# An attention pair's fine scores beside the next pair's coarse ones, and new costs for the planner of a two-stage kernel

## The chip, the cores and the metric

The kernel runs on one core of a Trainium2 chip. Its engines work side by side, each through its own queue in order: TensorE (PE in the profile; PEld is its weight load), VectorE (DVE), ScalarE (ACT), GpSimd (POOL), and SyncE (SP), which here issues all DMAs. The metric is device time in microseconds of one execution.

## The reference, cut to what matters

```python
B, H, S, D = 8, 8, 576, 64                   # q, k, v are (B, H, S, D) float32
q_d, k_d, v_d = (x.reshape(B, H, 144, 4, D).mean(axis=3) for x in (q, k, v))
out_d  = sm_attn(q_d, k_d, v_d)              # softmax(q k^T / 8) v over 144 pooled positions
out_up = np.repeat(out_d, 4, axis=2)
mask   = np.abs(pos[:, None] - pos[None, :]) < 4
scores = np.where(mask, q @ k^T / 8, -1e9)   # a band of 7 positions
out_local = softmax(scores) @ v
x = (out_up + out_local).transpose(0, 2, 1, 3).reshape(4608, 512)
h = x @ w_in                                 # w_in (512, 2048)
y = (h - tanh(h)) @ w_out                    # w_out (2048, 512); y is the output
```

## The kernel before, in words

**Two stages.** The attention makes the 4608 x 512 matrix x, kept transposed as four tiles `xT` (one for each pair of heads, channels on partitions, all tokens beside each other). The dense stage multiplies it by w_in and w_out in 9 blocks of 512 tokens.

**Attention.** 64 heads are worked off as 32 pairs, four pairs to a batch, two pairs to a group (16 groups). For a group, q and k are loaded in four DMAs to `qkn` (`load_qk`), cast to bf16 with an exchange of axes (`reorder`, L441: q and k apart, i = 0 and 1), transposed on TensorE (`turn`, L457, nine matmuls), copied out of PSUM to `qk` (L463), and pooled by two adds, `half` (L473) and `qkd` (L478). For pair p, `attention(p)` then runs: `s1`, the band scores of four of the five query tiles (8 matmuls, L508); exp of them (L547, 128x960) and multiplication by the 0/1 mask (L551); `s2`, the band scores of the fifth tile and the pooled scores (6 matmuls, L508 and L527); exps of these (L562, 128x192, and L565, 128x576) and a small mask (L569); `outs`, 18 matmuls of the probabilities by v and pooled v (L580, L586); reciprocal (L595) and scaling to `ln` (L597). Up to pair 11 `ln` is transposed on TensorE (`back`, L631 to L635), copied by ScalarE (`od`, L638) and added to `xT` by VectorE (L640). From pair 12 (`XOUT`) on a DMA transposes it and VectorE adds the two parts (L616).

**PSUM.** Two tiles of two banks each, `ps_ts` and `ps_ox`, serve the attention ("ts" and "ox" in the code; the first batch has a second pair of them), four banks `ps_hy` the dense stage. Up to pair 13, `s1` and `s2` of a pair are two operations that both write `ps_ts`. From pair 14 (`MERGE`) on they are one operation, `both`, which writes `s1` to `ps_ts` and `s2` to `ps_ox`.

**Dense.** `mm1` (L663) makes a 128 x 512 piece of h from four matmuls; ScalarE takes tanh (L672), VectorE subtracts to `gT` (L675). `mm2` (L691) accumulates 16 matmuls to a 128 x 512 piece of y; ScalarE copies it (L702) and SyncE stores it (L705).

**Weights** come as float32 in eight quarters (`load_w`), are kept in tiles that are free at that time (`gT`, and a part of `xT`), and are cast in pieces of 128 x 512 (L397). The queue of loads is: groups 0 and 1 and their v, w_in, groups 2 and 3, w_out, groups 4 and on. From group 9 on, a load waits until pair 2n - 5 has issued its output transpose (the key `fl`, with `AHEAD` = 5).

**What sets the order.** Nothing is issued as it is written. Each step is registered with `op(engine, ns, function, reads, writes, pri)`, or with `choice` where several engines could do it (casts, copies, adders). `Program.order` then plays the whole program through: it takes for each engine the ready step of the lowest `pri`, lets it last its `ns`, and lets users on other engines start after the engine's `LAT` (L25). The order of these planned starts is the order in which the instructions are put into the engines' queues; on the chip semaphores make them wait for their inputs, and nothing passes another in a queue. Dense matmuls have `pri` 5000, so they fill what attention leaves on TensorE. `spare` (L32, L243) adds to the lag for steps of high `pri`: 2500 ns after a DMA and 1000 ns after POOL, from `pri` 140 on. `pri` is 10 for each pair or 20 for each group. In `load`, the DMA's cost is the planned transfer time (`T_QK`, `T_V`, `T_W`; transfers are planned one behind the other). In gaps of TensorE before the first dense matmul, `filler` (L867) puts matmuls on a tile `warm`, whose result nobody reads.

**The loop** over pairs (L836 on) registers, for each p, the values' cast, scores, the transposes of group n + 1 where `INNER` and `OUTER` say so (from pair 8 on the one with i = p % 2), outputs, and at odd p the next group's loads; after each batch it registers the dense blocks that have become possible.

Of the kernel before, what the change touches and what calls it, by code (L numbers as in the profile page):

```python
# [9 lines left out]
BF16 = mybir.dt.bfloat16  # L10
# [5 lines left out]
class Program:  # L16
# [10 lines left out]
    def __init__(self):  # L27
        self.ops = []
        self.alternatives = {}
        self.touch = []  # L30
        self.fresh = set()
        self.spare = (5000, {})  # L32
        self.last_write = {}
        self.readers = {}
# [27 lines left out]
    def order(self):  # L62
# [16 lines left out]
        for _ in range(n):  # L79
            best = None  # L80
            for eng, cand in ready.items():
                if not cand:
                    continue
                now = max(free.get(eng, 0.0), min(at[i] for i in cand))
                if eng == "DMA":
                    pick = min((at[i], i) for i in cand)[1]
                else:
                    pick = min((self.ops[i][4], i) for i in cand if at[i] <= now)[1]
                if best is None or now < best[0]:
                    best = (now, eng, pick)  # L90
            now, eng, i = best
            if i in self.alternatives:
                for other in self.alternatives[i]:
                    ready[other].remove(i)
                self.ops[i] = self.alternatives[i][eng] + self.ops[i][3:]
            else:
                ready[eng].remove(i)
            start[i] = now
            end = now + self.ops[i][1]
            free[eng] = end  # L100
            for u in users[i]:
                same = self.ops[u][0] == eng and eng != "DMA"
                lag = self.LAT[eng]
                if self.spare[0] <= self.ops[u][4] < 5000:
                    lag += self.spare[1].get(eng, 0)
                at[u] = max(at[u], end if same else end + lag)
                left[u] -= 1
                if left[u] == 0:
                    make_ready(u)
# [45 lines left out]
def kernel(  # L155
# [9 lines left out]
    nc = tc.nc  # L165
# [76 lines left out]
    P = Program()  # L242
    P.spare = (140, {"DMA": 2500, "POOL": 1000})  # L243
    op = P.op
# [50 lines left out]
    def load(ns, fn, keys, cost, pri, after=()):  # L295
        op("SP", ns, fn, reads=after, writes=list(keys) + ["queue", ("q", keys[0])],
           pri=pri)
        op("DMA", cost, None, reads=[("q", keys[0])], writes=keys, pri=pri)

    def slot_qk(n):  # L300
        return n % 2 if n >= GV else n % NQKN

    def load_v4(n):

        b, h0 = n // 2, 4 * (n % 2)
        base = v[b, h0]
        for i, (g0, m) in enumerate(((0, 128), (128, 16))):
            rows = bass.AP(tensor=base.tensor, offset=base.offset + 4 * D * g0,
                           ap=[[4 * D, m], [S * D, 4], [1, 4 * D]])
            to = v4[128 - m:128, i]  # L310
            load(650, lambda to=to, rows=rows: nc.sync.dma_start(out=to, in_=rows),
                 [("qkn", 2, i, y) for y in range(2)], (1100, 350)[i], -30,
                 [("fl", 2 * n - AHEAD)])
# [18 lines left out]
    def load_qk(n):  # L332

        b, h0, s = n // 2, 4 * (n % 2), slot_qk(n)
        for i, src in enumerate((q, k)):
            for y in range(2):
# [7 lines left out]
                def issue(to=to, rows=rows):  # L344
                    nc.sync.dma_start(out=to, in_=rows)  # L345
                load(650, issue, [("qkn", s, i, y)], T_QK, -30,
                     [("fl", 2 * n - AHEAD)])

    def load_v(p):

        b, j, s = p // NP, p % NP, p % NVST
        t = vst[s]
# [24 lines left out]
    def load_w(src, dst, name, f, stage, keys):  # L377

        def issue():
# [4 lines left out]
            else:  # L384
# [4 lines left out]
                else:  # L389
                    nc.sync.dma_start(  # L390
                        out=stage.rearrange("p (c f) -> p c f", c=4),
                        in_=rows[:, 4 * f:4 * f + 4, :])
        load(600, issue, keys, T_W, -30)
        for c in range(4):
# [7 lines left out]
    def prep_v(p):  # L402
        s, w, jj = p % NVST, (p // 2) % NVW, p % 2
        P.choice([(eng, ns, lambda fn=fn: fn(  # L404
# [5 lines left out]
    def pool_v(hb):  # L410
# [6 lines left out]
        def mm():  # L417
# [7 lines left out]
           writes=[key], pri=pri)  # L425
        op("ACT", 300, lambda: A.copy(
            out=vd[w][:, :, :, 0:64],
# [18 lines left out]
    def turn(n, i):  # L446
# [5 lines left out]
        pri, cold = 20 * n, (1.5 if n < 1 else 1.0)  # L452
        b16 = ps.rearrange("p n c -> p (n c)").bitcast(BF16)[:, 0:A6 * 128]

        def tr():
            for a in range(A6):
                T.transpose(b16[:, 128 * a:128 * a + 128], qr[s][:, i, a, :], ident)  # L457
        P.fresh.add(len(P.ops))
        op("PE", 480 * cold, tr, reads=[("qr", s, i), "ident"], writes=ts, pri=pri)
        o = qk[s][:, :, KOFF * i:KOFF * i + 576]  # L460
# [15 lines left out]
        def add2(eng):  # L476
            with nc.allow_low_precision("pooled q and k"):
# [4 lines left out]
        P.choice([(name, n2, lambda eng=eng: add2(eng)) for name, _, n2, eng in adders],  # L482
                 reads=["half"], writes=[("qkd", s, i)], pri=pri)

    def attention(p):
# [43 lines left out]
        qks = [("qk", sq, i) for i in range(2)]  # L529
        pad = ["bias", "ident"] if first else []  # L530
        yield
        P.fresh.add(len(P.ops))
        if first:
            op("PE", 480, lambda: off(0, 480, 0), reads=pad, writes=ts, pri=pri)
        qkds = [("qkd", sq, i) for i in range(2)]
        if p >= MERGE:
            def both():
                s1()
                s2()
            op("PE", 800, both, reads=qks + qkds, writes=ts + ox, pri=pri)  # L540
        else:
            op("PE", 420 * cold, s1, reads=qks, writes=ts, pri=pri)
# [7 lines left out]
        if not first:  # L550
            op("DVE", 700, lambda: V.tensor_tensor(  # L551
                out=e1, in0=e1,
# [4 lines left out]
        if first:  # L557
            op("PE", 100, lambda: off(480, 96, 0), reads=pad, writes=ts, pri=pri)
        if p < MERGE:
            op("PE", 380 * cold, s2, reads=qks + qkds, writes=ts, pri=pri)  # L560
        sb = ox if p >= MERGE else ts
# [6 lines left out]
        if not first:  # L568
            op("DVE", 220, lambda: V.tensor_tensor(  # L569
                out=e2v, in0=e2v,  # L570
# [111 lines left out]
    def mm2(kb, i):  # L682
# [16 lines left out]
        if part == 3:  # L699
# [7 lines left out]
               reads=[("y", ys)], writes=[("yq", ys)], pri=-1)  # L707
            op("DMA", 1000, None, reads=[("yq", ys), ("y", ys)], pri=-1)

    def dense(kb):  # L710
# [13 lines left out]
        for i in range(16):  # L724
            if kb < NBLK:
# [4 lines left out]
    M2_FIRST = 16  # L730
    XOUT, T_OUT, AHEAD = 12, 2000, 5
    MERGE, GV = 14, 7
    XADD = [("DVE", (800, 350), V)]
    ORDER, W_FIRST = "g0123", "0123g"
    INNER, OUTER = {4: [0], 5: [1]}, {3: [0, 1], 7: [0, 1]}
    T_QK, T_V, T_W, W_PRI, NEARLY = 760, 800, 2750, 33, NP
    CAST = [("POOL", 700, GP.tensor_copy), ("ACT", 520, A.copy)]
    CAST_V = [[("POOL", 720, GP.tensor_copy), ("ACT", 640, A.copy)],
              [("POOL", 790, GP.tensor_copy)]]
    any3 = [("DVE", 860, V.tensor_copy), ("ACT", 950, A.copy),  # L740
            ("POOL", 1350, GP.tensor_copy)]
    REORDER = [[any3, any3], [any3[0:1], any3[2:3]]]
    TURN = [[("ACT", 1125, A.copy), ("DVE", 1250, V.tensor_copy)],
            [("ACT", 1125, A.copy)]]
    ADDERS = [[("DVE", 750, 440, V), ("POOL", 1190, 750, GP)],
              [("POOL", 1190, 880, GP)]]
# [89 lines left out]
    for p in range(NPAIR):  # L836
# [5 lines left out]
        if p >= 2:  # L842
            next(work[p])
        inner = INNER.get(p, [p % 2] if p >= 2 * NP else [])
        outer = OUTER.get(p, [])
        for i in inner if n + 1 < NGRP else []:
            reorder(n + 1, i)
            turn(n + 1, i)
        next(work[p], None)
        for i in outer:  # L850
            reorder(n + 1, i)
            turn(n + 1, i)
        if p % 2 == 1:
# [47 lines left out]
```

## Time and profile before

| | |
|---|---|
| median of 13 runs | 344.22 us (343.2 to 348.7) |
| the profiled execution: time, span | 345.8 us, 344.1 us |
| mean granted clock of TensorE in it | 0.978 |
| `mm1` and `mm2` matmuls, busy (records overlap) | 144.6 and 141.6 us |
| tanh L672, subtraction L675 | 0.600 us and 0.685 us each, 144 of each |
| DMA, 0 to 94 us; after that | share near 1.0; 0.06 to 1.04 |
| POOL's last work | about 250 us |

The page divides the span into 40 slices of 8.6 us. A digit is the busy share of a slice in tenths; in the row PEclk it is the granted clock of TensorE. A row of windows gives the stretch, its length, the busy time with the number of instructions of each engine asked for, the granted clock, the DMA share and GB/s. A row of waits reads: who waited for whom, total us, how often, the longest. In a timeline the columns are start, duration (of several instructions: from the first start to the last end), engine, line, operation, output and input, count, and in brackets how long the engine had been idle and what ended it. Matmuls of TensorE overlap; a matmul's record is longer than the distance to the next.

### The profile page before, as it was taken

What the parts mean: (1) busy time and instruction counts of PE and PEld (TensorE: products, weight loads), DVE (VectorE), ACT (ScalarE), POOL (GpSimd) and SP (SyncE); (2) the same over time, 40 slices, a digit from 0 to 9 for tenths busy, and PEclk for the clock granted to TensorE, in tenths of its full rate; (3) what the DMA queues carried; (4) which work ended last, traced back from release to release, by engine and by line L of the source; (5) the groups of instructions that cost most, each with busy time, mean ns of one, the idle gap of its engine ahead of it and who ended that gap; (6) DMA issues with size and microseconds to landing.
All of it is one profiled execution on the core that took longest, in us unless ns stands there. A gap on an engine that the chain in (4) does not pass through costs nothing.

```text
span 344.1 us, 6786 instructions
## 1 busy us (share of the span) xinstructions
PE 323.4 (94%) x2570; PEld 169.4 (49%) x2616; DVE 214.4 (62%) x360; ACT 204.7 (60%) x342; POOL 152.3 (44%) x179
## 2 busy tenths in 40 slices
PE   4886999998999999999999999999999999999995
PEld 1562554554565554545455555454544444444442
DVE  4766674658997678678676668766676453344300
ACT  2675897558868575756667656665765244344411
POOL 8434865595885066748483838492300000000000
PEclk9696999999999999999999999999999999999999
DMA  7998999999902397969898869862222200100021
GB/s 218 257 388 261 246 337 326 259 291 284 289 17 58 105 253 217 224 164 213 225 180 227 188 178 221 222 175 59 59 57 60 57 30 32 60 32 32 30 85 68
DMA packets 84749, 57.51 MB, mean 167 GB/s; under 512 B 62638, under 2 KB 67822, under 8 KB 84718
## 3 DMA queue, kind: packets, MB, share of 16 engines
q1 hardware_dynamic: 84718, 57.09, 60.8%
q8 instruction: 20, 0.33, 0.4%
q14 instruction: 11, 0.09, 0.1%
HBM read 43.05 MB, written 9.44 MB: 153 GB/s over the span
## 4 chain that ended last, share of the span: by engine, by line
PE 79%; DMA 10%; DVE 3%; SPq 3%; ACT 2%; issue 2%; ACTq 0%; DVEq 0%
PE ps_hy L663 33%; PE ps_hy L691 33%; DMA qkn<-in_q_dram 6%; PE ps_ts L457 3%; DMA gT<-in_moe_w_in_dram 3%; PE ps_ts L508 2%; PE ps_ox L580 2%; PE ps_ox L586 2%; SPq L369 2%; DMA qkn<-in_k_dram 1%; DVE ln L597 1%; SPq L345 1%; ACT uy L672 1%; PE ps_ox L527 1%; DVE qr L441 1%
## 5 line engine op out<-in xcount | busy, mean ns | idle before, releaser
L663 PE MATMUL ps_hy<-xT,w_in_sb 128*128 128x512 bf16 x555 | 144.6, 383 | 5.6 <-DVE xT L640 3.7
L691 PE MATMUL ps_hy<-w_out_sb,gT 128*128 128x512 bf16 x552 | 141.6, 379 | 2.1 <-issue 1.1
L675 DVE TENSOR_TENSOR gT<-ps_hy,uy 128x512 bf16<-128x512 f32 x144 | 95.8, 685 | 57.0 <-ACT uy L672 56.3
L672 ACT ACTIVATE uy<-ps_hy 128x512 f32<-128x512 f32 x144 | 83.8, 600 | 78.5 <-PE ps_hy L663 76.5
L663 PEld LDWEIGHTS <-w_in_sb 128*128 128x128 bf16 x576 | 53.9, 99 | 64.0 <-issue 7.3
L691 PEld LDWEIGHTS <-gT 128*128 128x128 bf16 x576 | 53.4, 98 | 59.7 <-issue 0.3
L473 POOL TENSOR_TENSOR half<-qk 128x576 f32<-128x576 bf16 x29 | 34.6, 1193 | 57.3 <-ACT qk L463 56.6
L463 ACT COPY qk<-ps_ts 128x1152 bf16<-128x1152 bf16 x28 | 31.5, 1126 | 15.6 <-PE ps_ts L457 13.5
L702 ACT COPY uy<-ps_hy 128x512 f32<-128x512 f32 x36 | 21.2, 588 | 21.7 <-PE ps_hy L691 20.7
L597 DVE TENSOR_TENSOR ln<-ps_ox,r 128x896 bf16<-128x896 f32 x30 | 32.7, 1090 | 0.9
L547 ACT ACTIVATE E<-ps_ts 128x960 bf16<-128x960 f32 x30 | 29.2, 974 | 6.8 <-PE ps_ts L508 6.7
L551 DVE TENSOR_TENSOR E<-E,mask 128x960 bf16<-128x960 bf16 x28 | 22.1, 789 | 11.1 <-ACT E L547 10.7
L404 POOL CAST vw<-vst 128x640 bf16<-128x640 f32 x31 | 24.0, 785 | 9.5 <-DMA vst<-in_v_dram 7.8
L457 PEld LDWEIGHTS <-qr 128*128 128x128 bf16 x288 | 20.1, 104 | 12.7 <-DVE qr L441 5.6
L322 POOL TENSOR_TENSOR qkn<-qkn 128x512 f32<-128x512 f32 (+1 forms) x18 | 24.1, 1337 | 4.3 <-DMA qkn<-in_v_dram 3.2
L441 DVE CAST qr<-qkn 128x1152 bf16<-128x1152 f32 x18 | 15.8, 877 | 13.1 <-DMA qkn<-in_q_dram 9.8
L478 POOL TENSOR_TENSOR qkd<-half 128x288 bf16<-128x288 f32 x30 | 22.5, 750 | 2.4 <-DVE half L473 1.3
L457 PE MATMUL ps_ts<-ident,qr 128*128 128x128 bf16 x252 | 19.1, 222 | 4.1 <-DVE qr L441 2.6
L441 POOL CAST qr<-qkn 128x1152 bf16<-128x1152 f32 x14 | 17.0, 1218 | 8.1 <-DMA qkn<-in_k_dram 7.7
L616 DVE TENSOR_TENSOR xT<-lnT 128x480 bf16<-128x480 bf16 (+1 forms) x40 | 20.6, 528 | 0.0
L595 DVE RECIPROCAL r<-ps_ox 128x14 f32<-128x14 f32 x30 | 7.3, 243 | 20.8 <-PE ps_ox L586 18.9
L580 PE MATMUL ps_ox<-vw,E 128*128 128x65 bf16 x300 | 18.4, 194 | 1.0 <-DVE E L569 1.0
(86 smaller groups left out, 252.5 us busy)
## 6 DMA issues: line engine op xcount, KB each, us to landing
vst<-in_v_dram SPq DMA_DIRECT2D x62, 160.0 KB, 5.2
qkn<-in_q_dram SPq DMA_DIRECT2D x32, 288.0 KB, 3.5
qkn<-in_k_dram SPq DMA_DIRECT2D x32, 288.0 KB, 4.9
out_dram<-uy SPq DMA_DIRECT2D x36, 256.0 KB, 2.0
qkn<-in_v_dram SPq DMA_DIRECT2D x9, 512.0 KB, 5.3
gT<-in_moe_w_in_dram SPq DMA_DIRECT2D x4, 1024.0 KB, 11.8
xT<-in_moe_w_out_dram SPq DMA_DIRECT2D x8, 256.0 KB, 5.3
gT<-in_moe_w_out_dram SPq DMA_DIRECT2D x2, 1024.0 KB, 10.7
```

The costliest lines, as they stand in the source:

```text
L322: op("POOL", 1330, lambda t=t: GP.tensor_tensor(out=t[:, :, 0:2], in0=t[:, :, 0:2], in1=t[:, :, 2:4], op=ALU.add), writes=keys, pri=pri)
L441: P.choice([(eng, ns, lambda fn=fn: fn(out=dst, in_=srt)) for eng, ns, fn in REORDER[n >= 2][i]], reads=[("qkn", sn, i, x) for x in range(2)],
L457: T.transpose(b16[:, 128 * a:128 * a + 128], qr[s][:, i, a, :], ident)
L463: fn(out=o.rearrange("p y (g a) -> p y g a", a=A6), in_=b16.rearrange("p (a g y) -> p y g a", a=A6, y=2))
L473: eng.tensor_tensor(out=half, in0=four[:, :, :, 0:2], in1=four[:, :, :, 2:4], op=ALU.add)
L547: op("ACT", 980, lambda: A.activation(out=e1, in_=ps[:, :, 0:480], func=AF.Exp, scale=SCALE), reads=ts, writes=[("E", se, 0)], pri=pri)
L580: T.matmul(po[:, hh, 65 * t:65 * t + 65], E[se][:, c:c + 128], vw[w][:, 2 * jj + hh, t, :], start=True, stop=True)
L597: op("DVE", 1090, lambda: V.tensor_tensor(out=ln[sl].rearrange("p n (h d) -> p h n d", d=D), in0=blocks[:, :, :, 0:64], in1=r[s].unsqueeze ...
L663: T.matmul(ps_hy[slot], w_in_sb[:, dc, fc * 128:(fc + 1) * 128], xT[dc][:, kb * 512:kb * 512 + 512], start=(dc == 0), stop=(dc == N_DC - 1))
L672: op("ACT", 490, lambda: A.activation(out=u[us], in_=ps_hy[slot], func=AF.Tanh), reads=[("hy", slot)], writes=[("u", us)], pri=-1)
L675: op("DVE", 620, lambda: V.tensor_tensor(out=gT[g][:, fc, :], in0=ps_hy[slot], in1=u[us], op=ALU.subtract), reads=[("hy", slot), ("u", us) ...
L691: T.matmul(ps_hy[slot], gT[g][:, fc, ts * 128:ts * 128 + 128], w_out_sb[:, fc, :], start=(fc == 0), stop=(fc == N_FF - 1))
```

## The change

1. `MERGE` goes from 14 to 12, and the merged block is another one. From pair 12 on, `both` holds `s1` of pair p + 1 (to `ps_ts`) and `s2` of pair p (to `ps_ox`). Pair 12's own `s1` stands alone, and so does the last pair's `s2`.
2. From pair 12 on, the transposes of a group are registered earlier (`EARLY` = 12): both of group 7 at pair 12, and from there i = 0 of group n + 2 at odd pairs, and i = 1 of group n + 1 at even pairs, where before group n + 1 had one at each.
3. `spare` becomes a function of priority, engine and user. After a DMA: 1500 ns from `pri` 80 on, 2500 from 140. For users on TensorE, from `pri` 120 and from 180: POOL 1000 and 1500, VectorE 300 and 800, ScalarE 200 and 500. For other users: POOL 500 and 1000.
4. Planned costs change: q and k loads 760 to 900 (the k loads of group 0 by 400 more), v 800 to 780, the first two quarters of w_in by 300 and 1400 more, pooled v's loads, output stores 1000 to 750, output transposes 2000 to 1600, the masks 700 to 900 and 220 to 450, several casts and copies.
5. VectorE becomes a choice for the weights' casts.
6. A way to transpose q and k by DMA is added for groups from `FI` on, with a function `slot_v`; `FI` is 99, and there are 16 groups.

In the queues that result, the weights' 32 casts stand 15 on POOL, 9 on ScalarE, 8 on VectorE (before 18, 14, 0); the 32 casts of q and k 17 on POOL and 15 on VectorE (before 14 and 18); 18 filler matmuls (before 10). Every other matmul is there as before. The order of the loads on SyncE is the same; stores stand differently among them.

```diff
-    P.spare = (140, {"DMA": 2500, "POOL": 1000})
+    def spare(pri, eng, to):
+        if eng == "DMA":
+            return 2500 if pri >= 140 else 1500 if pri >= 80 else 0
+        level = (pri >= 120) + (pri >= LATER)
+        return SPARE[to == "PE"].get(eng, (0, 0, 0))[level]
+    LATER = 180
+    SPARE = ({"POOL": (0, 500, 1000)},
+             {"POOL": (0, 1000, 1500), "DVE": (0, 300, 800), "ACT": (0, 200, 500)})
...
+    def slot_v(p):
+        return p % 4 if p >= 2 * FI else p % NVST
...
-                load(650, issue, [("qkn", s, i, y)], T_QK, -30,
+                load(650, issue, [("qkn", s, i, y)],
+                     T_QK + (400 if n == 0 and i == 1 else 0), -30,
...
-        load(600, issue, keys, T_W, -30)
+        load(600, issue, keys, T_W + (W_LATE[f] if src is moe_w_in else 0), -30)
...
-        op("ACT", 300, lambda: A.copy(
+        op("ACT", 600, lambda: A.copy(
...
+        if n >= FI:
+            op("SP", 900, lambda: nc.sync.dma_start_transpose(
...
+        if n < FI:
+            P.fresh.add(len(P.ops))
+            op("PE", 480 * cold, tr, reads=[("qr", s, i), "ident"], writes=ts, pri=pri)
...
+        nexts[p] = s1, qks
...
-        if p >= MERGE:
-            def both():
-                s1()
-                s2()
-            op("PE", 800, both, reads=qks + qkds, writes=ts + ox, pri=pri)
-        else:
+        if p <= MERGE:
             op("PE", 420 * cold, s1, reads=qks, writes=ts, pri=pri)
...
-            op("DVE", 700, lambda: V.tensor_tensor(
+            op("DVE", 900, lambda: V.tensor_tensor(
...
-        if p < MERGE:
-            op("PE", 380 * cold, s2, reads=qks + qkds, writes=ts, pri=pri)
+        if MERGE <= p < NPAIR - 1:
+            ahead, more = nexts[p + 1]
+
+            def both():
+                ahead()
+                s2()
+            op("PE", 800, both, reads=qks + qkds + more, writes=ts + ox, pri=pri)
+        else:
+            op("PE", 380 * cold, s2, reads=qks + qkds, writes=ox if p >= MERGE else ts,
+               pri=pri)
...
-    XOUT, T_OUT, AHEAD = 12, 2000, 5
-    MERGE, GV = 14, 7
+    XOUT, T_OUT, AHEAD = 12, 1600, 5
+    MERGE, GV = 12, 7
+    FI, T_IN, EARLY = 99, 2050, 12
...
-    T_QK, T_V, T_W, W_PRI, NEARLY = 760, 800, 2750, 33, NP
-    CAST = [("POOL", 700, GP.tensor_copy), ("ACT", 520, A.copy)]
+    W_LATE = [300, 1400, 0, 0]
+    T_QK, T_V, T_W, W_PRI, NEARLY = 900, 780, 2750, 33, NP
+    CAST = [("POOL", 620, GP.tensor_copy), ("ACT", 620, A.copy),
+            ("DVE", 400, V.tensor_copy)]
...
-        inner = INNER.get(p, [p % 2] if p >= 2 * NP else [])
-        outer = OUTER.get(p, [])
+        inner = INNER.get(p, [] if p < 2 * NP else [p % 2] if p < EARLY else
+                          [0, 1] if p == EARLY else [1] if p % 2 == 0 else [])
+        m = n + 1 + (p > EARLY)
+        outer = OUTER.get(p, [0] if p > EARLY and p % 2 else [])
```

## The prediction

> **What bounds the kernel now.** I read the page's table of slices first, then stages by windows, then TensorE's waits and the timelines around them. The profiled execution took 345.8 us (its span is 344.1); the median of the 13 runs is 344.22, so that execution is 1.6 us above it. My sum is made against 345.8 and its difference carried to 344.22.
>
> ```profile
> span 344.1 us, 6786 instructions
> PE 323.4 (94%) x2570; PEld 169.4 (49%) x2616; DVE 214.4 (62%) x360; ACT 204.7 (60%) x342; POOL 152.3 (44%) x179
> PE   4886999998999999999999999999999999999995
> PEclk9696999999999999999999999999999999999999
> ```
> ```profile
> 36.00:82.00 46.00, 42.78 (x397) 1.00 1.01 290
> 82.00:262.00 180.00, 177.72 (x1560) 1.00 0.66 167
> 262.00:344.00 82.00, 77.19 (x367) 0.99 0.14 49
> ```
>
> TensorE has work nearly always. A dense matmul starts every 0.216 us ("0.86 us for x4" in the chain), so the 1152 of them alone need 249 us, and the order of TensorE's queue is fixed by the planner. The time is therefore TensorE's work plus the places where its next instruction is not ready. From 82 to 262 us (a row of the second fence: busy 177.7 of 180) I find only missing records, no waits. The losses are in three places: the start up to 36 us; three waits between 57 and 80 us; one at 275 us.
>
> The middle:
>
> ```profile
> PE ps_ox L580 <- DVE E L569: 1.0, 1, 1.0
> PE ps_ox L631 <- DVE ln L597: 0.9, 1, 0.9
> PE ps_ts L508 <- ACT qk L463: 0.7, 1, 0.7
> ```
> ```profile
> 58.10 1.02 DVE L441 CAST qr<-qkn 128x1152 bf16<-128x1152 f32 x1 [2.91 <-DMA qkn<-in_q_dram]
> ...
> 59.31 1.09 DVE L597 TENSOR_TENSOR ln<-ps_ox,r 128x896 bf16<-128x896 f32 x1
> ...
> 60.46 0.23 PE L631 MATMUL ps_ox<-ident,ln 128*128 128x128 bf16 x1 [0.95 <-DVE ln L597]
> ```
>
> VectorE stood 2.91 us in front of a cast whose load had not landed; pair 5's `ln`, whose input was ready before 57 us, was queued behind it, and TensorE waited 0.95 us. The other two have the same root or a like one: a cast waiting 2.87 us for q from 75.45 to 78.32 us holds up the mask of pair 8 (1.0 us lost), and a full-width `half` on POOL, queued behind a memset of 0.95 us, holds up ScalarE's `qk` copy (0.7 us lost). Together **2.6 us**.
>
> **The early start.** Weights, not TensorE, set it:
>
> ```profile
> 25.05 0.62 ACT L397 CAST w_in_sb<-gT 128x512 bf16<-128x512 f32 x1 [2.10 <-DMA gT<-in_moe_w_in_dram]
> ...
> 25.57 0.27 ACT L638 COPY od<-ps_ox 128x144 bf16<-128x144 bf16 x1
> ...
> 25.88 0.76 DVE L640 TENSOR_TENSOR xT<-ps_ox,od 128x576 bf16<-128x576 bf16 x1 [0.97 <-ACT od L638]
> ...
> 27.39 0.81 PE L663 MATMUL ps_hy<-xT,w_in_sb 128*128 128x512 bf16 x2 [2.54 <-DVE xT L640]
> ```
>
> ScalarE stands at a cast of the second quarter of w_in until it lands at 25.03; the `od` copy of pair 1 waits behind it, then `xT`, then the first dense matmul. The same happens again with the third quarter (landed 27.74): `od` of pair 3 at 29.63, eight dense matmuls from 30.75.
>
> **The change, part by part.**
>
> *Planned load times.* With its costs laid end to end, the planner of before expects the third and fourth quarter of w_out at 46.9 and 49.7 us and group 4's q and k from 50.5 to 52.7. The trace lands them at 53.9, 56.6 and 57.3 to 59.7: six or seven us late. With the new costs the plan has 51.1, 53.9 and 54.8 to 57.5, and from group 4 on (priority 80 and more) 1.5 us of slack on top. In the changed order of VectorE the cast of group 4's q stands behind `ln` of pair 5 and both masks of pair 6 (before: in front of pair 5's `ln`), that of group 6 behind `ln` of pair 7 (before: in front of it), that of group 7 behind the `ln` of pair 8 and the large mask of pair 9 (before: in front of pair 8's second mask). On POOL the memset now stands behind group 4's first `half`. All three waits lose their cause: -2.6. What is late next: TensorE comes 2.6 us earlier to group 5 and later; group 5's first transpose stands at dense matmul 124, about 70 us, its q landed by 63.4; group 6's at 168, about 83 us, landed by 73. Hidden.
>
> *w_in and the start.* The changed queues still hold a w_in cast in front of `od`: on ScalarE one of the second quarter, then `od` of pairs 2 and 1, then two of the third, then `od` of pair 3; VectorE has one of the second quarter ahead of `r` of pair 3. By the rows above: landing 25.03, cast to 25.65, `od` 2 and 1 to 26.25, `xT` of 2 and 1 to about 27.5 (2 x 0.76), `ln` of pair 3 to 28.6, its transposes to 29.0, `od` behind the casts of the third quarter (27.76 + 2 x 0.57 = 28.9), `xT` to between 30.1 and 30.7. The first dense matmul at 27.5 instead of 27.39, the steady run from 30.2 to 30.7 instead of 30.75: **0**, ends +0.3 and -0.6. That q and k casts move from VectorE (0.76) to POOL (1.14) and ScalarE's copies (1.12) to VectorE (1.36) at the start lies in front of the same landing; cover of at least 2 us.
>
> *Eight more filler matmuls* (18 for 10), all before the first dense one. Row: the granted clock is 0.50 from 8.2 to 15.0 us, after a stretch (4.8 to 8.2) with 1.11 of 3.40 us busy; again 0.50 from 28.7 to 35.5, after 0.79 of 3.40. [...] I take 0 for both.
>
> *Merged blocks from pair 12 on, fine scores of p beside coarse scores of p+1.* The same matmuls; two pairs more without a separate entry, about 0.1 us each: -0.2. The wait that matters is from the block to the pair's outputs (`O`). Before, 10 to 16 dense matmuls stand between, most often 12 and a transpose, as the big exp (0.97) and mask (0.79) must fit. Now 6 to 12, at the tightest 8, or 6 and a transpose: 0.22 + 8 x 0.216 = 1.95 us from the fine scores' start. The chain to fit is now only the small exps and the small mask. Nearest row: pair 4, fine scores at 44.23, exps ended 45.44, `O` at 46.19 after the same distance: 0.76 us spare. One dense evacuation in front (tanh 0.60, subtraction 0.685) still fits. Cost 0; ends 0 and +7 (third rival).
>
> *Earlier transposes after pair 12* (up to 72 dense matmuls earlier). Loads of group n still wait for the output transpose of pair 2n-5. Row: that pair's `O` at 161.25, transpose issued 163.48, q landed 168.9, k 171.8; with a cast (0.88 and 1.22) 8.5 and 11.8 us. The changed distance is at least 52 dense matmuls to the q transpose (11.2 us) and 64 to the k one (13.8), not counting the attention between. Hidden with 2 us to spare; if that is gone, TensorE waits the excess once per group, seven times.
>
> *End of attention.* The last `O` stands at dense matmul 786 instead of 810, the block that needs it still at 836: cover grows from 26 to 50 matmuls, 10.8 us. In the trace the short cover makes the planner bunch 14 L663 matmuls at 275 us, and
>
> ```profile
> 275.59 3.46 PE L663 MATMUL ps_hy<-xT,w_in_sb 128*128 128x512 bf16 x14 [0.67 <-ACT uy L702]
> ```
>
> The changed order has the regular alternation there: **-0.8** (0.67, and the stumble before and after it).
>
> *A new tight place.* At dense matmul 214 pair 11's back-transposes are followed by only a transpose, two matmuls and the pooling (1.6 us) before a matmul that needs its `xT` (`od` 0.28, `xT` 0.76, two hand-overs, 1.2 or more with VectorE's queue). Between 0 and +0.8; I take +0.2.
>
> *Dead parts.* FI = 99 is above the 16 groups: the DMA transpose of q and k is never emitted, and `slot_v` is p % 6 as before.
>
> Sum: -2.6 + 0 + 0 - 0.2 - 0.8 + 0.2 = **-3.4**: 342.4 for the profiled execution, 340.8 for the median.
>
> **The rivals.** (1) *Main case*, 340.8, own range 339.3 to 342.5: chance 0.55. [...] 0.15. (3) *The loads decide anyway*: DMA is at a share of 1.01 from 36 to 82 us, so TensorE, once early, waits for groups 5 to 7; only the 1 us of the end and merges remains, 343.2. Against it: the spare of 6 us and more at groups 5 and 6. 0.12. (4) *Slower: merged blocks too close to the outputs.* Place: the 20 `O` blocks of pairs 12 to 31. If a `qk` copy (1.12 us) stands ahead of the small exps in ScalarE's queue, the 0.76 us are overdrawn by about 0.36; at a mean 0.35, 20 x 0.35 = 7.0, and 340.8 + 7.0 = 347.8. It decides above a mean of 0.17 us per block (3.4 / 20). For it: such copies are one per pair, and ScalarE is busy 107 of 165 us there. Against it: slack planned for TensorE's inputs, 0.2 to 0.5 us from ScalarE and 0.3 to 0.8 from VectorE. 0.18.
>
> **How the numbers follow.** 0.3% is 1.0 us, about what a measurement of this kernel can tell from no change. Faster: nearly all of (1), (2), half of (3): 0.74. Same: 0.07. Slower: (4) with a little of the rest: 0.19. The range 337.3 to 345.5 takes in (2) and (3), the ends of the start and of pair 11, and the milder half of (4).
>
> **What would show it.** TensorE's three waits between 57 and 80 us gone, and no VectorE cast that waits over 1 us with `ln` or a mask behind it; no dense matmul that waits for a copy of L702 near 270; the first run of eight and more dense matmuls still near 30.5 us and a half-clock stretch there; the waits of `O` for exps and masks from pair 12 on below 1 us in all. The forecast is wrong if those waits sum to over 3 us, if waits for q, k or v appear between 60 and 90 us, or if the dense run begins before 29 or after 32 us.

## The result, and the profile after

The changed kernel takes **341.58 us** (median of 11 runs, 339.82 to 343.49); the kernel before, timed beside it, takes 344.9 (48 runs). The ratio is **0.9895, 95% interval 0.9873 to 0.9918**. The forecast, 340.8 against 344.22, was a ratio of 0.990. The profiled execution took 341.42 us (span 339.7, granted clock 0.995), where that of before took 345.8 (344.1, 0.978). One run of a later kernel (`merge_undone`, 428.15 us at a mean clock of 0.754) was in a slow state and is left out of its median.

The page's head, its row of engines and two rows of its table of slices, after:

```profile
span 339.7 us, 6802 instructions
PE 323.4 (95%) x2578; PEld 168.3 (50%) x2624; DVE 229.6 (68%) x369; ACT 199.6 (59%) x334; POOL 157.2 (46%) x178
PE   7786999999999999999999999999999999999995
PEclk9997999999999999999999999999999999999999
```

TensorE's busy time is the same to a tenth of a microsecond; the span has lost 4.4 us of idle or half-clock time. In the PEclk row the two dips of before (6 in the second slice, 6 in the fourth) have become one 7 in the fourth. The row says nothing of the first 9.26 us, where the trace's record of the clock has not begun: nine transposes that take 1.14 us at 5.87 us and 0.67 at 9.51 show TensorE at half speed there. Mean clocks leave out such a head too (0.995 is what the one stretch of 3.4 us at half clock, 29.74 to 33.15, makes of the record behind 9.26 us). The windows, with TensorE alone:

```profile
36.00:82.00 46.00, 45.11 (x426) 1.00 0.98 280
82.00:262.00 180.00, 177.52 (x1555) 1.00 0.68 171
262.00:344.00 82.00, 73.64 (x336) 0.99 0.12 43
```

From 36 to 82 us TensorE's idle time is 0.9 us instead of 3.2. From 82 to 262 the 2.5 us without a record are mostly missing records: another execution of the same program, taken later, has 32 records more there and this window table:

```profile
36.00:82.00 46.00, 45.83 (x432) 1.00 1.00 283
82.00:262.00 180.00, 179.66 (x1587) 1.00 0.69 169
```

TensorE works 225.5 of 226 us. What is left is the start, and 3.7 us at the end (77.5 us from 262 to the span's end, 73.8 busy), while the last results are copied and stored. TensorE's waits say the same. First 36 to 82 us (before: 1.0, 0.9 and 0.7 us for E, `ln` and `qk`), then 82 to 262 us, in the first changed profile:

```profile
PE ps_hy L692 <- issue: 0.3, 2, 0.2
PE ps_hy L720 <- issue: 0.2, 1, 0.2
```
```profile
PE ps_ox L432 <- DVE xT L669: 0.3, 1, 0.3
PE ps_ox L609 <- DVE E L598: 0.2, 1, 0.2
PE ps_hy L720 <- issue: 0.2, 1, 0.2
PE ps_hy L692 <- issue: 0.2, 1, 0.2
```

All three waits of the middle are gone. `O` (L609 now) waited once for a mask, 0.2 us. At the end of the attention the two dense products alternate and nothing waits for an evacuation (timeline of TensorE, after; before, 14 matmuls stood together at 275.59 behind a wait of 0.67):

```profile
272.82 1.89 PE L720 MATMUL ps_hy<-w_out_sb,gT 128*128 128x512 bf16 x8
274.55 1.89 PE L692 MATMUL ps_hy<-xT,w_in_sb 128*128 128x512 bf16 x8
276.27 1.03 PE L720 MATMUL ps_hy<-w_out_sb,gT 128*128 128x512 bf16 x4
```

The start, pair 3's way to the dense run (timeline of all engines, after):

```profile
27.14 1.08 DVE L626 TENSOR_TENSOR ln<-ps_ts,r 128x896 bf16<-128x896 f32 x1
28.28 0.23 PE L660 MATMUL ps_ts<-ident,ln 128*128 128x128 bf16 x1 [0.63 <-DVE ln L626]
...
28.90 0.28 ACT L667 COPY od<-ps_ts 128x144 bf16<-128x144 bf16 x1 [1.11 <-PE ps_ts L664]
29.22 0.76 DVE L669 TENSOR_TENSOR xT<-ps_ts,od 128x576 bf16<-128x576 bf16 x1 [0.99 <-ACT od L667]
...
30.03 4.93 PE L692 MATMUL ps_hy<-xT,w_in_sb 128*128 128x512 bf16 x15 [1.21 <-POOL w_in_sb L410]
```

From the two `xT` before this `ln` on, these are the steps of the prediction, with one difference: `od` of pair 3 waits 1.11 us for TensorE, while ScalarE's casts of the third quarter, which the prediction put in front of it, had ended at 27.79. (In the last row the profile names a cast by POOL from 29.37 to 29.98; `xT` ends at 29.98 too, and that cast is of the fourth quarter, which the first pieces do not read.) The dense run starts 0.2 us before the forecast's earliest end (30.2) and 0.7 us before that of the kernel before (30.75). The second and third quarter of w_in landed at 23.92 and 26.63 instead of 25.03 and 27.74, and the half-clock stretch behind was 3.4 us long (29.74 to 33.15) instead of 6.8. Is that the change's doing? The last group of experiments answers it.

### The profile page after: what moved, and what is told of

Read it like the earlier page. It is cut to its first block, busy times and chain, and to the rows that moved or that the text cites. A ratio compares the mean times of both kernels' runs of the same rounds, so it can differ in the third digit from the quotient of the medians.

```text
span 339.7 us, 6802 instructions
## 1 busy us (share of the span) xinstructions
PE 323.4 (95%) x2578; PEld 168.3 (50%) x2624; DVE 229.6 (68%) x369; ACT 199.6 (59%) x334; POOL 157.2 (46%) x178
## 4 chain that ended last, share of the span: by engine, by line
PE 82%; DMA 5%; DVE 5%; SPq 3%; issue 2%; ACT 1%; POOL 1%; ACTq 0%; POOLq 0%; DVEq 0%
PE ps_hy L720 35%; PE ps_hy L692 33%; PE ps_ts L479 4%; DMA gT<-in_moe_w_in_dram 4%; PE ps_ts L533 3%; PE ps_ox L609 3%; PE ps_ox L615 2%; SPq L382 2%; DMA qkn<-in_k_dram 2%; DVE gT L704 1%; DVE xT L645 1%; DVE E L572 1%; PE ps_ox L432 1%; DVE qr L454 1%; PE ps_ox L552 1%
## 5 line engine op out<-in xcount | busy, mean ns | idle before, releaser
L701 ACT ACTIVATE uy<-ps_hy 128x512 f32<-128x512 f32 x144 | 83.1, 600 | 69.2 <-PE ps_hy L692 64.2
L486 ACT COPY qk<-ps_ts 128x1152 bf16<-128x1152 bf16 x26 | 29.2, 1125 | 9.7 <-PE ps_ts L479 8.9
L731 ACT COPY uy<-ps_hy 128x512 f32<-128x512 f32 x36 | 21.2, 588 | 18.3 <-PE ps_hy L720 17.6
L454 POOL CAST qr<-qkn 128x1152 bf16<-128x1152 f32 x17 | 21.4, 1258 | 18.8 <-DMA qkn<-in_k_dram 16.0
L572 DVE TENSOR_TENSOR E<-E,mask 128x960 bf16<-128x960 bf16 x28 | 24.9, 890 | 5.0 <-ACT E L568 4.9
L645 DVE TENSOR_TENSOR xT<-lnT 128x480 bf16<-128x480 bf16 (+1 forms) x40 | 23.8, 611 | 0.0
L479 PEld LDWEIGHTS <-qr 128*128 128x128 bf16 x288 | 18.4, 99 | 10.2 <-DVE qr L454 2.9
L598 DVE TENSOR_TENSOR E<-E,mask 128x192 bf16<-128x192 bf16 x28 | 13.8, 494 | 10.8 <-ACT E L591 10.7
L609 PE MATMUL ps_ox<-vw,E 128*128 128x65 bf16 x300 | 18.3, 194 | 0.2 <-DVE E L598 0.2
L609 PEld LDWEIGHTS <-E 128*128 128x128 bf16 x300 | 15.4, 98 | 6.2 <-DVE E L598 0.3
```

Source lines behind the costliest of these rows:

```text
L486: fn(out=o.rearrange("p y (g a) -> p y g a", a=A6), in_=b16.rearrange("p (a g y) -> p y g a", a=A6, y=2))
L572: op("DVE", 900, lambda: V.tensor_tensor(out=e1, in0=e1, in1=mask[:, 0:480].unsqueeze(1).to_broadcast([128, 2, 480]), op=ALU.mult), reads= ...
L609: T.matmul(po[:, hh, 65 * t:65 * t + 65], E[se][:, c:c + 128], vw[w][:, 2 * jj + hh, t, :], start=True, stop=True)
L645: up=up: eng.tensor_tensor(out=xo[:, QW * t0:QW * t0 + nt * n].rearrange("p (t g a) -> p t g a", t=nt, a=4), in0=lnT[sl][:, t0:t0 + nt, 0: ...
L701: op("ACT", 490, lambda: A.activation(out=u[us], in_=ps_hy[slot], func=AF.Tanh), reads=[("hy", slot)], writes=[("u", us)], pri=-1)
```

## The experiments

**Which part brings the gain.** Five kernels take the change apart. The first is the kernel before with nothing but the new costs of loads (item 4 of the change, its first half) and the slack after a DMA from priority 80 on:

```diff
-    P.spare = (140, {"DMA": 2500, "POOL": 1000})
+    def spare(pri, eng):
+        if eng == "DMA":
+            return 2500 if pri >= 140 else 1500 if pri >= 80 else 0
+        return 1000 if eng == "POOL" and pri >= 140 else 0
...
-    T_QK, T_V, T_W, W_PRI, NEARLY = 760, 800, 2750, 33, NP
+    T_QK, T_V, T_W, W_PRI, NEARLY = 900, 780, 2750, 33, NP
```

> The kernel before with the new load costs alone (q and k 900, v 780, pooled v 1800 and 250, w_in later by 300 and 1400, k of group 0 by 400, and 1.5 us of slack after a DMA from priority 80 on); blocks, casts and the slack for TensorE as before. Load-time theory: the three waits of TensorE between 57 and 80 us go (2.6 us), the stumble at the end (0.8) stays: 342.3 against 344.9, ratio 0.992. Theory that the merged blocks bring the gain: 344.9, ratio 1.00. Theory that the clock at the start brings it: 344.9, unless fillers and idle time at the start change too; the granted clock from 8 to 15 us tells that.

343.14 us (342.5 to 344.51), ratio 0.9954 (0.9933 to 0.9975): somewhat over half of what was expected (0.46% less time, expected 0.8%), and the stumble at the end, expected to stay, is gone. TensorE's windows:

```profile
36.00:82.00 46.00, 44.46 (x422) 1.00 1.03 300
82.00:262.00 180.00, 176.53 (x1547) 1.00 0.67 163
```

The middle loses 1.5 us where before lost 3.2; but 82 to 262 us has 1.0 us less of records than the changed kernel's profile with nearly as many (1547 and 1555), and TensorE waits there 0.7 us for `ln` and 0.6 for a mask, which it does not in before. The load costs take the middle's waits away and open smaller ones behind.

Second, the changed kernel with the old costs of loads (the edit above in reverse, `W_LATE`, pooled v's costs and the 400 for the k loads of group 0 with it):

> The changed kernel with the old load costs (the same numbers set back, slack after a DMA only from priority 140). Load-time theory: waits of VectorE for q and of TensorE behind them come back between 55 and 85 us, 2 to 3 us in all: 344, ratio 0.997. Theory of the merged blocks: 341.6 as the changed kernel, ratio 0.99.

349.05 us, ratio 1.0133 (1.0111 to 1.0155): well above the expectation, and slower than before. TensorE's waits from 36 to 82 us, then from 82 to 262:

```profile
PE ps_ts L533 <- ACT qk L486: 1.3, 1, 1.3
PE ps_hy L692 <- DVE gT L704: 1.3, 1, 1.3
PE ps_hy L692 <- ACT uy L731: 0.5, 1, 0.5
```
```profile
PE ps_ox L660 <- DVE ln L626: 1.3, 1, 1.3
PE ps_ox L432 <- DVE xT L669: 0.7, 1, 0.7
PE ps_hy L692 <- DVE gT L704: 0.6, 1, 0.6
```

Not one wait but several, of the same kind as in before (`ln`, `qk`) and new ones for the dense evacuations. The prediction's mechanism stands in front of one of them (timeline of VectorE): behind this cast the subtraction to `gT` comes late, and TensorE waits for it for 1.32 us at 79.76:

```profile
78.34 0.76 DVE L454 CAST qr<-qkn 128x1152 bf16<-128x1152 f32 x1 [5.03 <-DMA qkn<-in_q_dram]
```

At the end the bunch of 14 matmuls is back (timeline of TensorE), although this kernel has the earlier transposes:

```profile
278.31 3.46 PE L692 MATMUL ps_hy<-xT,w_in_sb 128*128 128x512 bf16 x14 [0.67 <-ACT uy L731]
```

Third, the changed kernel with all old costs and slack, so that of the change only the merged blocks and earlier transposes are left:

> The changed kernel with all costs, slacks and choices of engines of before; the new merged blocks from pair 12 and the earlier transposes stay. Load-time theory: the waits of 57 to 80 us stay, the last outputs come earlier relative to the dense stage and the stumble near 275 us goes: about 1 us faster than before, 343.9, ratio 0.997. Theory of the merged blocks: most of the gain, 341.6 to 342.2, ratio 0.991. Slower-rival (blocks too close to the outputs): waits of the outputs for exps or masks from pair 12 on, since the slack for TensorE is gone, up to 348.

350.38 us, ratio 1.0173 (1.0139 to 1.0207). The time is near that of the prediction's slower rival (347.8), but the rival's mechanism, in the first row of TensorE's waits from 82 to 262 us, is only a part of it:

```profile
PE ps_ox L606 <- DVE E L595: 2.3, 4, 1.3
PE ps_ts L476 <- DVE qr L451: 1.0, 3, 0.5
PE ps_hy L717 <- issue: 1.0, 6, 0.2
```

`O` (L606 here) waits four times for the small mask, 2.3 us in all, where the changed kernel waits 0.2. A fifth wait, of 1.76 us at 77.45, has the cause of the kernel before, a cast in front of its load with the mask behind it (timeline of VectorE):

```profile
76.47 0.76 DVE L451 CAST qr<-qkn 128x1152 bf16<-128x1152 f32 x1 [3.91 <-DMA qkn<-in_q_dram]
77.14 0.25 DVE L595 TENSOR_TENSOR E<-E,mask 128x192 bf16<-128x192 bf16 x1
```

The rest of the loss is spread: transposes wait for casts of q and k (1.0 here), and a second half-clock stretch stands from 78.2 to 81.6 us.

Fourth, the changed kernel with its costs and slack, but blocks and transposes in the form of before (`MERGE` = 14, `both` holding `s1` and `s2` of the same pair, `EARLY` = 99):

> The changed kernel with the merged blocks and the places of the transposes set back to the form of before (from pair 14, both scores of the same pair); all new costs and slacks stay. Load-time theory: the middle stays free of waits, so most of the gain stays: 342 to 342.5, ratio 0.993; the stumble at the end, gone in the kernel with the new load costs alone as well, stays away. Theory that blocks and costs only work together: 344 or more, ratio 1.00.

349.54 us (348.91 to 350.48, 5 runs), ratio 1.0156 (1.0122 to 1.0189): the new costs in full, on the old blocks, are worse than the old ones. The middle is as good as in the changed kernel; the loss lies behind (a row of windows, then TensorE's waits from 82 to 262 us, and one of them in the timeline of TensorE):

```profile
36.00:82.00 46.00, 45.11 (x428) 1.00 0.97 282
82.00:262.00 180.00, 172.87 (x1486) 1.00 0.67 167
```
```profile
PE ps_hy L689 <- DVE gT L701: 2.7, 4, 0.9
PE ps_ts L479 <- ACT E L573: 1.3, 3, 0.5
PE ps_hy L689 <- ACT uy L728: 0.7, 4, 0.2
```
```profile
141.78 1.02 PE L689 MATMUL ps_hy<-xT,w_in_sb 128*128 128x512 bf16 x4 [0.92 <-DVE gT L701]
```

Small waits that return with every group: the dense stage's PSUM comes free late, as VectorE's subtraction stands behind a cast of q (1.08 us at 140.05). These rows show 4.7 of the 7.1 us that have no record; how much of the rest is missing records, this profile can't tell. The stumble at the end, expected to stay away, is back (0.67 us at 279.21).

Fifth, only the earlier transposes undone, the merged blocks kept:

```diff
-    FI, T_IN, EARLY = 99, 2050, 12
+    FI, T_IN, EARLY = 99, 2050, 99
```

> The changed kernel with the transposes of the last pairs planned as before and all else as changed (merged blocks, new costs, slack). If the blocks are what the new costs need (undoing blocks and transposes together gave 349.8): 341 to 342.5 us, idle time of PE in 82 to 262 us near 2.5 us. If the earlier transposes are: 346 us or more, with 5 us or more of idle time there.

343.52 us (343.0 to 344.56, 12 runs), ratio 0.996 (0.9945 to 0.9975); the changed kernel beside it 341.46. Neither expectation: beside the new costs the blocks carry most of it, the transposes about 2 us. `O` waits for masks again, 3.1 us in two places, and the larger one is no matter of the blocks (timeline of all engines):

```profile
54.22 1.18 DVE L410 CAST w_out_sb<-gT 128x512 bf16<-128x512 f32 x2 [1.79 <-DMA gT<-in_moe_w_out_dram]
...
55.31 0.72 DVE L598 TENSOR_TENSOR E<-E,mask 128x192 bf16<-128x192 bf16 x1
...
56.08 0.20 PE L609 MATMUL ps_ox<-vw,E 128*128 128x65 bf16 x1 [2.00 <-DVE E L598]
```

VectorE stands 1.79 us in front of a cast whose quarter of w_out has not landed, the mask behind it, TensorE behind the mask: the pattern of the kernel before, with another load. An edit that begins at pair 12 has moved work that runs long before it, because the planner lays out the whole program again.

**The slack for TensorE's users.** The changed kernel with one slack for all:

```diff
-             {"POOL": (0, 1000, 1500), "DVE": (0, 300, 800), "ACT": (0, 200, 500)})
+             {"POOL": (0, 500, 1000)})
```

> The changed kernel with no extra slack for users on TensorE from VectorE and ScalarE, and POOL's 500 and 1000 for them as for others. Theory that the slack carries the merged blocks: the outputs wait for exps and masks from pair 12 on, as in the kernel with the blocks alone (7.4 us idle from 82 to 262 us there, 2.5 in the changed kernel): 2 to 5 us more, 344 to 346. Theory that the real costs of masks and casts suffice: 341.6 to 342.3.

342.81 us (341.5 to 344.73, 12 runs), ratio 0.9961 (0.9939 to 0.9983); the changed kernel, run beside it, 342.06 and 0.9925 (0.9897 to 0.9953). The intervals overlap: the 0.75 us between them may be noise. TensorE's largest wait behind 36 us is 0.3 us in this profile, so no place can be named. `O` does not wait for masks: this slack is not what keeps the merged blocks from the slower rival.

**The fillers and the start.** First the changed kernel with 10 filler matmuls instead of 18; TensorE's other work keeps its order:

```diff
-                fill[i] = (name, int(0.75 * room / slow))
+                fill[i] = (name, min(int(0.75 * room / slow), 10 - sum(c for _, c in fill.values())))
```

> The changed kernel with 10 filler matmuls instead of 18 (the last 8 left out); they compute nothing that is read. Load-time theory: the start is set by the landing of w_in, so 341.6 as the changed kernel, ratio 0.990, even if the clock is at half from 8 to 15 us. Theory of the clock: the half-clock stretch of 6.8 us comes back and costs up to 2.8 us: 343 to 344.4, ratio 0.996.

339.59 us (338.66 to 340.11, 5 runs), ratio 0.9851 (0.9828 to 0.9874): faster, against the expectation, the clock 1.0 in four of the five. (The 2.8 us there is an estimate from the kernel before: half of the 5.52 us that TensorE is busy from 8.2 to 15.0 us, at a granted clock of 0.50.) To see whether idle time near 25 us decides the clock, the same kernel got 11 more matmuls with unread results between 23 and 30 us, where TensorE has nothing to do (four in front of pair 2's back-transposes, seven about the first dense piece):

> The changed kernel with the last 8 fillers left out and 11 others (their results are not read) put into the idle time from 23 to 30 us: 4 before the back-transposes of pair 2, 2 behind the first dense matmuls, 5 before the dense run at 30 us. Theory that the half-clock stretch around 30 us is what makes the changed kernel's runs spread from 339.8 to 343.5: it never occurs now, all runs within 338.5 to 340.2 and the clock 1.000. Theory that the missing fillers alone made the faster run: as that one, 339.6 (338.7 to 340.1), with a cold stretch in some.

339.80 us (339.26 to 340.42, 6 runs), ratio 0.9867 (0.9841 to 0.9892). Not faster than 10 fillers alone. The half-clock stretch near 30 us is absent from its profile, as expected, but there is one from 16.42 to 19.83 us, and the mean clock of the runs is 0.990 to 0.998, not 1.000. That idle time decides the clock is not shown by this. The changed kernel once more in the same round:

> The changed kernel itself once more, on the same chip as the runs beside it: 341.6 (ratio 0.990). Load-time theory and the others expect the same; it is the measure for the three kernels beside it.

342.06 us (339.09 to 343.2, 9 runs). Then 10 fillers a second time, the changed kernel a third time, and it without any filler (the diff's line replaced by `pass`), all in one round:

> The changed kernel with 10 fillers in place of 18, a second time. If fewer fillers keep the clock up between 24 and 30 us: 339 to 340 us again, mean clock 0.995 or more in most runs. If the first time was luck with the clock: 341 to 342 us, with the clock spread from 0.983 to 1.0 as in the changed kernel, and the same time as that at the same clock.

> The changed kernel once more, beside the run with 10 fillers: 341.5 us, single runs from 339 to 343.5, each 0.01 of mean clock worth 1.9 us.

> The changed kernel with no filler matmuls at all, the order of all other work kept. If the work before 24 us has time to spare before the dense layer's first weights land: 340 to 341.5 us, PE slower until some 12 us, dense run from 30 us on as before. If the cold start reaches the end: 343 us or more.

Ten fillers: 341.45 (339.42 to 342.79, 6 runs), ratio 0.9889 (0.9859 to 0.9918). The changed kernel: 341.46 (339.86 to 343.37, 6 runs), 0.9902 (0.9869 to 0.9935). So the first result with ten was most likely the clock's luck. No filler: **340.02 (339.84 to 340.33, 4 runs), 0.9853 (0.983 to 0.9877)**. It is no slower than with 18, the interval says a little faster; after the lesson with ten I call four runs in a row no proof of that. The timeline of TensorE without fillers:

```profile
5.87 1.14 PE L479 MATMUL ps_ts<-ident,qr 128*128 128x128 bf16 x9 [5.87 <-POOL vd L797]
...
14.29 1.14 PE L479 MATMUL ps_ox<-ident,qr 128*128 128x128 bf16 x9
...
29.61 4.65 PE L692 MATMUL ps_hy<-xT,w_in_sb 128*128 128x512 bf16 x13 [1.20 <-DVE xT L669]
```

The nine transposes at 14.29 last 1.14 us (the changed kernel's at 13.37: 0.68), and the clock's record begins only at 16.22 us. Yet the dense run starts at 29.61, no later than with fillers. What covers the slow start is not the landing of w_in. Followed back from 29.61, the chain is `xT`, `od` and the back-transposes of pair 3, then VectorE without a gap from the `r` before `ln` of pair 2 on (22.52 us), then TensorE's outputs, and at 16.79 a matmul that had waited for POOL's cast of v. In front of that one the fillers change nothing here: with 18 it starts at 16.76. The third quarter of w_in, landed at 26.42, holds nothing on this chain, since `od` of pair 3 waits for TensorE and not behind ScalarE's casts (first row, timeline of ScalarE without fillers).

Half speed behind that point does cost time. In the second execution with ten fillers the clock was at half from 16.58 to 19.99 us, and VectorE waited for TensorE (second row, timeline of VectorE); in the first one it waited 0.63 us there:

```profile
28.49 0.28 ACT L667 COPY od<-ps_ts 128x144 bf16<-128x144 bf16 x1 [0.91 <-PE ps_ts L664]
20.76 0.25 DVE L624 RECIPROCAL r<-ps_ox 128x14 f32<-128x14 f32 x1 [2.18 <-PE ps_ox L615]
```

Its third quarter landed early (26.24), but its dense run started at 30.84, 1.0 us later than in the first. So 18, 10 or no fillers made no difference that these runs can tell from the clock's.

The traces also show where the spread comes from. These six executions run the same work on TensorE in the same order, so the times of one step can be compared. "21st" and "last" are the starts of the 21st and the 180th evacuation of a dense result (L701 and L731 together); all times in us, read from the traces:

| kernel | third quarter of w_in lands | `ln` of pair 2 | dense run | half clock, 24 to 36 us | 21st | last | between |
|---|---|---|---|---|---|---|---|
| after | 26.63 | 23.36 | 30.03 | 29.74-33.15 | 74.37 | 336.09 | 261.72 |
| after, second | 27.92 | 24.64 | 32.26 | 25.65-29.06, 32.48-35.89 | 76.63 | 337.60 | 260.97 |
| after, third | 25.95 | 22.19 | 28.97 | 27.95-34.77 | 74.82 | 335.87 | 261.05 |
| 10 fillers | 26.46 | 23.16 | 29.82 | none | 73.26 | 334.22 | 260.96 |
| 10 fillers, again | 26.24 | 24.18 | 30.84 | 30.23-33.64 | 75.20 | 336.56 | 261.36 |
| no filler | 26.42 | 22.94 | 29.61 | 29.87-33.28 | 73.99 | 334.96 | 260.96 |

Behind the 21st evacuation all six need 261.0 to 261.7 us. In front of it they differ by 3.4 us: by the start of the dense run and by how much of it falls into a half-clock stretch (0 to 5.8 us of it, at half speed). The start does not follow the third quarter's landing, and `od` of pair 3 waits 0.7 to 1.5 us for TensorE in all six. It follows `ln` of pair 2: 6.7 to 6.8 us from there in five of the six, and 7.6 in the second of after, where TensorE was at half clock from 25.65. What sets that `ln` differs: in the second of after a VectorE cast that had waited 2.44 us for the first quarter of w_in (landed by 22.52), in the second with ten fillers TensorE's half-clock stretch. The timed runs go with the clock as well: of 27 runs of the changed kernel, those with a mean clock of 0.999 or more have a median of 339.8 us (3), of 0.992 to 0.996 340.7 (7), of 0.990 or less 342.3 (17); a straight line through the 27 gives 1.9 us for each 0.01 of mean clock.

## Why the prediction was right

**The total.** Forecast 340.8, measured 341.58; the forecast ratio of 0.990 lies in the measured interval.

**The middle (-2.6).** Right: the three waits of 2.6 us are down to none over 0.3. That the load costs are needed is shown from both sides: alone on the kernel before they halve the idle time of 36 to 82 us (3.2 to 1.5 us), taken out of the changed kernel it is 3.6. They are not enough for every order: without the earlier transposes a wait of 2.0 us stands there again, behind a cast in front of its load.

**The end of the attention (-0.8).** Right: the bunch of 14 matmuls and its wait of 0.67 are gone. But the step put it down to the longer cover of the earlier transposes; the kernel with load costs alone, which does not have them, shows no wait there either, and the changed kernel with the old load costs, which has them, shows the same bunch of 14 and the 0.67. So the longer cover neither is needed nor suffices; the number came out of another layout of the plan, and why the planner bunches there stays open.

**The start (0).** The order of the steps was right, but not what holds them. "Weights, not TensorE, set it" is true of the kernel before, where VectorE's `xT` waits for an `od` behind a cast of the second quarter (landed 25.03). Already there `od` of pair 3 waited 0.73 us for TensorE, not for the third quarter, as the prediction read it. In the changed kernel the chain runs through VectorE's queue and TensorE, and neither the second nor the third quarter is on it. That the term of 0 fits is luck in this. The profiled pair shows about -1.5: 0.7 from the earlier dense run, 0.8, an estimate, from that run's share at a granted clock of 0.50 (3.12 us, 30.03 to 33.15, instead of 4.75, 30.75 to 35.5; half of the difference). Three executions of the one changed program start the dense run at 30.03, 32.26 and 28.97, on both sides of the 30.75 of before, so a pair of profiles cannot tell a term of 1.5 us here from 0. The range should have held this: its ends for the start, +0.3 and -0.6, were taken from the order of queues alone, as if loads landed at the same time and the clock stood the same in every execution.

**The fillers (0).** Right in size: no filler at all costs nothing in four runs (340.02 us; 341.46 with 18, beside them). But no run shows what a filler is worth, and the landing of w_in, by which the load-time theory expected no loss, is not what covers the slow start. With 18 fillers the half speed ended at 9.26 us in the first profile, before (10 fillers) at 15.0, though each is one execution and neither shows that the fillers end it. Nor is the time gained: TensorE's matmul at 16.8 us waits for POOL's cast of v with and without fillers (16.76 and 16.79), so what is faster in front of it is lost again.

**The second half-clock stretch (0: it stays).** Right as a tendency, but nothing fixed: from 24 to 36 us the clock was at half for none, 3.4 or 6.8 us. In before it cost 2.4 us by an estimate (half of the 4.75 us from 30.75 to 35.5, all busy at a granted clock of 0.50). At a mean clock of 1.0 the changed kernel took 339.1 and 339.8 us, in single executions. What decides whether the stretch comes, no run shows: from 24 to 30 us TensorE was busy 2.83 of 6 us in the first profile of after, which has it, and 3.01 in the first with ten fillers, which does not. The steps of the clock's record lie 3.41 us or a multiple apart within each execution (6.83, 13.65 and 6.83 us from 8.2 to 35.5 in before), and at another place in each (29.74, 25.65, 27.95 us above).

**The merged blocks (-0.2) and earlier transposes (0).** Here only the total of all terms was right, and these two were not: that is luck. The prediction priced each as if the rest of the order stood still. The runs give no such prices, nor the 0.1 us for a separate entry that the -0.2 was made of:

| kept of the change | us | ratio |
|---|---|---|
| load costs and DMA slack | 343.14 | 0.9954 |
| blocks and transposes | 350.38 | 1.0173 |
| all costs and slack | 349.54 | 1.0156 |
| all but load costs and DMA slack | 349.05 | 1.0133 |
| all but the earlier transposes | 343.52 | 0.9960 |
| everything | 341.58 | 0.9895 |

Taken as edits that add up, blocks and transposes are about +5.5 us on the old costs and -8.0 on the new (350.38 - 344.9, 341.58 - 349.54; the rounds differ, the kernel before took 344.4 to 345.1 in the later ones). The earlier transposes, costed 0 as "hidden", are worth 2; the larger of the two waits that come back without them (2.0 of 3.1 us) is at 56 us, long before the first of them.

**The rivals.** Loads that decide anyway: fell, no wait for q, k or v from 36 us on. Blocks too close to the outputs: fell for the change (0.2 us), but a part of it happens when the costs are the old ones (2.3 us of waits for masks in four places; the rival had 7.0), so the chance of 0.18 was no pessimism. What holds it off is not the slack for TensorE's users alone, which the prediction named against it; which of the other costs (masks 700 to 900 and 220 to 450, casts, VectorE as a choice) was not tried.

**Pair 11 (+0.2).** The back-transposes' `xT` holds no dense matmul up. There is one wait of 0.34 us for an `xT`, at 101.5 us, by pooling matmuls. Inside its bounds.

## What to carry to other kernels

Where a planner orders the queues, its costs and the operations it orders are one object: test parts of a change in both directions (alone, and left out), and parts that lose singly can win together. In a queue in order, place casts by when their load really lands; a cast that is planned too early holds up every step behind it (2.91 us from 55.2 to 58.10 in before, pair 5's `ln` behind it), and 2.6 us of TensorE's waits came from two loads and a memset. Before a step is said to wait for a load, look at what ended its engine's idle time: here the landing was near, and TensorE was what was waited for. And before a difference in the start of two profiles is believed, take the same program several times.

## What was not expected of the hardware

The landing of one and the same load, the third quarter of w_in, varied by 2.0 us between executions of kernels that issue their loads in the same order (25.95 to 27.92 us). TensorE's start varied more (28.97 to 32.26) and did not follow it. And the gain depends on the clock: at a mean clock of 0.999 or more the changed kernel takes 339.1 to 340.4 us (3 runs), at 0.990 or less 341.0 to 343.5 (17), while the kernel before moved less with it: in three later rounds 343.9 to 345.4 at 0.999 or more (3 runs, median 344.1), and 343.5 to 347.4 at 0.990 or less (47, median 344.7). That its waits in the middle take up what the start loses would explain this; it is argued, not shown.
